# Causal masks as TensorE matmuls, and an instruction order read from a table

## The chip, the core and the metric

The kernel runs on one core of a Trainium2 chip. Its engines are TensorE (PE: matmuls; its weight loads are listed apart as PEld), VectorE (DVE), ScalarE (ACT), GpSimd (POOL) and SyncE (SP, which issues the DMAs). Each works through its own queue strictly in order. The metric is the device time of one execution in microseconds; a time for a kernel is the median of several executions.

## The reference

```python
scores = scale * q @ k.T                          # 4 batches, 8 heads, 576 positions, 64 wide
mask = pos[:, None] // 64 >= pos[None, :] // 64   # causal by blocks of 64
attn = softmax(where(mask, scores, -1e9)); a = attn @ v
x = a.transpose(0, 2, 1, 3).reshape(2304, 512)
h = x @ w_in;  g = h * tanh(softplus(h));  x = g @ w_out    # Mish; 512 -> 2048 -> 512
h = maximum(x @ w_in2, 0);  out = (h * h) @ w_out2          # 512 -> 2048 -> 512
```

## The kernel before

**Work and passes.** Attention feeds a first two-matrix layer (Mish) and that feeds a second (squared ReLU). The 2304 tokens are cut into six chunks of 384, and the two layers run as twelve passes of one chunk each, in the order of `PASSES`: (layer 0, chunk 0), (0,1), (0,2), (1,0), (0,3), (1,1), (0,4), (0,5), (1,2), (1,3), (1,4), (1,5). A pass has 16 steps `f`. In each, `first_half` (L1156) makes one 128x384 tile `hp` of the hidden layer with 12 matmuls, ScalarE turns it into `h` (L1162), `g_parts` splits `h` into an f16 high and a low part (the high one on ScalarE, L981, or GpSimd, L982; the low one on VectorE, L692), and `second_half` (L1222) adds 12 matmuls into four accumulators. All operands but those of pass (0,0) are such pairs of f16, so that a product takes three matmuls. Pass (0,0) is computed in fp32 (`first_full`, L1176, Mish at L1181; `second_full`, L1191).

**Weights.** They come from DRAM in an 8-byte format. `decode` (L1000 to L1013) fetches a block `raw` and makes f32 `wf` of it, `weigh` (L1025, L1028) finds column norms with a square on ScalarE and a small matmul, `split` makes an f16 pair `wn` (L981 and L692) and writes it to DRAM (L1056). `weights` (L1073) fetches the pairs back into a ring of three buffers `ws` when a pass needs them.

**Attention.** For each pair of heads and each tile of 128 queries, `scores` (matmul at L780) issues six f16 matmuls into a PSUM tile `spare`: two heads, each with a sum of three products. A tile of queries spans two blocks, so its first 64 rows must not see the last 64 keys: VectorE overwrites these with a memset (L832; for the tile `i == 2`, that of the last queries' tail too, L835). Then `peak` (L788) takes the maximum, `expo` (L796) the exponentials, `finish` the f16 pair `pb` of the probabilities (L815 and, through `stt`, L692), which L819 transposes by DMA. `attention_lo` does the first queries of each head in fp32 and has its own memset (L918). `settle` (L891) puts the result into `xs`, `chunk_scale` (L1098 to L1122) makes the pair `x` of it (L1105 and L692) and the norms `nsq` (L1118 and L1119 on VectorE, then a matmul at L1120) that a pass needs before its first `h`.

**What sets the order.** The program records tasks (`sch.add`), each with an engine, a list of engines to choose from (`choose`), an estimated duration and the buffers it touches. `Sched.run` then runs a list scheduler (`forward`, `backward`) with estimated times; the 140 numbers of `SHIFT` pull single groups of tasks ahead or push them back. What comes out is the order of the instructions on every engine and the engine of each task with a choice. Mish and the exponential use different tables on ScalarE, so that a change from one to the other puts an `ACT_TABLE_LOAD` ahead of it. The rings (`Ring`) give a tile one of a fixed number of buffers in the order of recording; ring `us` (the weights' scales) has eight.

Of the kernel before, what the change touches and what calls it, by code (L numbers as in the profile page):

```python
# [85 lines left out]
SHIFT = {  # L86
    ('att', 0, 0): -9100, ('att', 0, 1): 69600, ('att', 0, 2): -8000, ('att', 0, 3): -7800,
    ('att', 0, 4): 2800, ('att', 0, 5): -3000, ('att', 0, 6): 43100, ('att', 0, 7): -16100,
    ('att', 1, 0): -20200, ('att', 1, 1): 38800, ('att', 1, 2): 23300, ('att', 1, 3): -42600,
    ('att', 1, 4): 51000, ('att', 1, 5): 600, ('att', 1, 6): 98300, ('att', 1, 7): 101100,  # L90
    ('att', 2, 0): 600, ('att', 2, 1): -300, ('att', 2, 3): 600, ('att', 3, 0): 7000,
    ('att', 3, 1): 500, ('att', 3, 2): 11400, ('att', 3, 3): 19000, ('att', 4, 0): -8500,
    ('att', 4, 1): 42600, ('att', 4, 2): 90600, ('att', 4, 3): 37600, ('att', 5, 0): -45800,
    ('att', 5, 1): 36700, ('att', 5, 2): -13200, ('att', 5, 3): 27200, ('av', 0, 0): -27300,
# [8 lines left out]
    ('decode', 0, 0, 1): -17200, ('decode', 0, 0, 2): 36800, ('decode', 0, 0, 3): 40300, ('decode', 0, 0, 4): -28500,  # L103
    ('decode', 0, 0, 5): 1400, ('decode', 0, 0, 6): -1100, ('decode', 0, 0, 7): -1300, ('decode', 0, 1, 0): 29500,
    ('decode', 0, 1, 1): 84600, ('decode', 0, 1, 2): 118100, ('decode', 0, 1, 3): -29600, ('decode', 0, 1, 4): -33900,
    ('decode', 0, 1, 5): -500, ('decode', 0, 1, 6): 2200, ('decode', 0, 1, 7): 400, ('decode', 1, 0, 0): 87300,
    ('decode', 1, 0, 1): -45900, ('decode', 1, 0, 2): 29600, ('decode', 1, 0, 3): 49200, ('decode', 1, 0, 4): 8500,
    ('decode', 1, 0, 5): -12600, ('decode', 1, 0, 6): -13400, ('decode', 1, 0, 7): 6700, ('decode', 1, 1, 0): -48800,
    ('decode', 1, 1, 1): -13400, ('decode', 1, 1, 2): -11700, ('decode', 1, 1, 3): -22400, ('decode', 1, 1, 4): -900,
    ('decode', 1, 1, 5): -8200, ('decode', 1, 1, 6): -1200, ('decode', 1, 1, 7): -2700, ('norm', 0, 1): -1300,  # L110
    ('norm', 0, 2): 18300, ('norm', 0, 3): -40400, ('norm', 0, 4): -86200, ('norm', 0, 5): -27500,
    ('norm', 1, 0): -800, ('norm', 1, 1): 43900, ('norm', 1, 2): -54900, ('norm', 1, 3): 24300,
    ('norm', 1, 4): -51600, ('norm', 1, 5): -60300, ('norms', 0, 0, 0): -400, ('norms', 0, 0, 4): -8900,
    ('norms', 0, 1, 0): -2200, ('norms', 0, 1, 4): -700, ('norms', 1, 0, 0): 1100, ('norms', 1, 0, 1): -23000,
    ('norms', 1, 0, 2): -8000, ('norms', 1, 0, 3): -300, ('norms', 1, 0, 4): 600, ('norms', 1, 0, 5): 800,
    ('norms', 1, 0, 6): -7400, ('norms', 1, 0, 7): -7300, ('norms', 1, 1, 0): 400, ('norms', 1, 1, 1): 30300,
    ('norms', 1, 1, 2): -8600, ('norms', 1, 1, 3): 2000, ('norms', 1, 1, 4): -9700, ('norms', 1, 1, 5): 14900,
    ('norms', 1, 1, 6): -12700, ('norms', 1, 1, 7): -20900, ('scale', 0, 1): -24700, ('scale', 0, 2): 400,
    ('scale', 0, 3): 31000, ('scale', 0, 4): -76700, ('scale', 0, 5): 31400, ('scale', 1, 0): -15400,
    ('scale', 1, 1): 300, ('scale', 1, 2): -30100, ('scale', 1, 3): -57800, ('scale', 1, 4): -12900,  # L120
    ('scale', 1, 5): -32100, ('split', 0, 0, 0): -26300, ('split', 0, 0, 1): -204500, ('split', 0, 0, 2): -68800,
    ('split', 0, 0, 3): -45600, ('split', 0, 0, 4): 27600, ('split', 0, 0, 5): 10500, ('split', 0, 0, 6): -1900,
    ('split', 0, 0, 7): 71500, ('split', 0, 1, 0): -47000, ('split', 0, 1, 1): -87900, ('split', 0, 1, 2): -5100,
    ('split', 0, 1, 3): 3700, ('split', 0, 1, 4): 79200, ('split', 0, 1, 5): 19000, ('split', 0, 1, 6): -2100,
    ('split', 0, 1, 7): 37100, ('split', 1, 0, 0): 58400, ('split', 1, 0, 1): 28400, ('split', 1, 0, 2): -7900,
    ('split', 1, 0, 3): 79300, ('split', 1, 0, 4): 11600, ('split', 1, 0, 5): -19400, ('split', 1, 0, 6): 3300,
    ('split', 1, 0, 7): -95400, ('split', 1, 1, 0): 24600, ('split', 1, 1, 1): -14200, ('split', 1, 1, 2): 24000,
    ('split', 1, 1, 3): -22100, ('split', 1, 1, 4): 22200, ('split', 1, 1, 5): 34400, ('split', 1, 1, 6): -86300,
    ('split', 1, 1, 7): -31800, ('weigh', 0, 0, 0): -50200, ('weigh', 0, 0, 1): -89800, ('weigh', 0, 0, 2): -39300,
    ('weigh', 0, 0, 3): -15300, ('weigh', 0, 0, 4): -13700, ('weigh', 0, 0, 5): 7900, ('weigh', 0, 0, 6): 9100,  # L130
    ('weigh', 0, 0, 7): 41100, ('weigh', 0, 1, 0): -56500, ('weigh', 0, 1, 1): -52200, ('weigh', 0, 1, 2): -10400,
    ('weigh', 0, 1, 3): 9300, ('weigh', 0, 1, 4): -29400, ('weigh', 0, 1, 5): -144800, ('weigh', 0, 1, 6): -24400,
    ('weigh', 0, 1, 7): -118800, ('weigh', 1, 0, 0): -27700, ('weigh', 1, 0, 1): 62600, ('weigh', 1, 0, 2): 25700,
    ('weigh', 1, 0, 3): -48500, ('weigh', 1, 0, 4): -1000, ('weigh', 1, 0, 5): 4000, ('weigh', 1, 0, 6): 77300,
    ('weigh', 1, 0, 7): 13100, ('weigh', 1, 1, 0): -100, ('weigh', 1, 1, 1): -2000, ('weigh', 1, 1, 2): 13300,
    ('weigh', 1, 1, 3): -26100, ('weigh', 1, 1, 4): -53300, ('weigh', 1, 1, 5): -33400, ('weigh', 1, 1, 6): 4800,
    ('weigh', 1, 1, 7): 142400,
# [1408 lines left out]
```

## Time and profile before

| | us |
| --- | --- |
| three executions | 954.25, 955.18, 955.38 |
| median | 955.18 |
| the profiled execution | 952.69 |
| its span in the trace | 950.9 |
| TensorE busy in it | 903.7 |
| VectorE busy | 593.8 |
| ScalarE busy | 623.3 |

The profiled execution's own time is 1.8 us more than the span of its trace, and 2.5 us less than the median. The rows below are of that one execution. In rows in order of time the columns are start, duration, engine, line, operation, out<-in; a bracket at the end is the idle time before it and what ended it.

### The profile page before, as it was taken

Reading aid. Unit: us, or ns where it says so; the run is one execution under the profiler, and the core shown is the slowest. Engines: PE = TensorE matmul, PEld = TensorE weight load, DVE = VectorE, ACT = ScalarE, POOL = GpSimd, SP = SyncE. Lnnn points to the kernel's source line nnn. Section 1 sums busy time; section 2 is a strip of 40 time slices with the busy share of each in tenths; the row PEclk is TensorE's granted clock in tenths of the full one; section 3 lists DMA queues with packets and bytes.
Section 4 is the critical chain, followed back from the end, with each engine's and each line's share of the span. In section 5 each row is a group of like instructions: output and inputs, shape, how many; then the busy total and the mean of one; then the engine's idle time right before and its main releaser. Section 6 shows DMA issues by size and latency. Waiting matters only on the chain. (4 is left out here: it accounts for less than half of the span.)

```text
span 950.9 us, 15602 instructions
## 1 busy us (share of the span) xinstructions
PE 903.7 (95%) x5674; PEld 530.6 (56%) x5674; DVE 593.8 (62%) x1449; ACT 623.3 (66%) x1166; POOL 103.0 (11%) x133
## 2 busy tenths in 40 slices
PE   7799997897989899999999999999999999999997
PEld 6455553454555555556556555555566666666664
DVE  6789999998999996453863387677751251331211
ACT  6789799999789876554894477577752242444442
POOL 0000101211223130000210021111200000000000
PEclk9899999799999999999999999999999999999999
DMA  9657586788768798493664268597642222333430
GB/s 344 242 183 291 200 205 165 175 258 241 287 206 250 257 251 248 135 245 115 179 158 124 101 145 236 167 251 173 178 123 74 69 70 68 109 135 133 166 112 33
DMA packets 141773, 168.79 MB, mean 178 GB/s; under 512 B 105856, under 2 KB 110976, under 8 KB 137600
## 3 DMA queue, kind: packets, MB, share of 16 engines
q1 hardware_dynamic: 141696, 167.80, 60.2%
q8 instruction: 44, 0.72, 0.3%
q14 instruction: 33, 0.27, 0.1%
HBM read 125.30 MB, written 17.30 MB: 150 GB/s over the span
## 5 line engine op out<-in xcount | busy, mean ns | idle before, releaser
L692 DVE SCALAR_TENSOR_TENSOR g<-h,cst,g 128x384 f16<-128x384 f32 x176 | 110.9, 632 | 250.1 <-ACT g L981 231.9
L1162 ACT ACTIVATE h<-hp,cst 128x384 f32<-128x384 f32 x176 | 101.4, 578 | 221.2 <-PE hp L1156 219.9
L1222 PE MATMUL acc<-g,ws 128*128 128x384 f16 x1128 | 231.3, 327 | 0.7 <-DVE g L692 0.7
L1222 PE MATMUL acc<-g,raw 128*128 128x384 f16 x984 | 206.9, 327 | 0.1
L1156 PE MATMUL hp<-x,first 128*128 128x384 f16 x768 | 162.9, 335 | 6.9 <-ACT h L1162 5.5
L1222 PEld LDWEIGHTS <-ws 128*128 128x128 f16 x1128 | 109.2, 98 | 75.6 <-issue 4.1
L1156 PEld LDWEIGHTS <-first 128*128 128x128 f16 x960 | 93.6, 99 | 82.6 <-issue 25.6
L1222 PEld LDWEIGHTS <-raw 128*128 128x128 f16 x984 | 95.6, 98 | 64.5 <-issue 1.6
L1156 PE MATMUL hp<-x,raw 128*128 128x384 f16 x552 | 118.7, 327 | 0.0
L982 POOL TENSOR_SCALAR g<-h,cst 128x384 f16<-128x384 f32 x66 | 54.8, 831 | 333.0 <-ACT h L1162 106.2
L1156 PE MATMUL hp<-x,ws 128*128 128x384 f16 x408 | 86.9, 331 | 0.8 <-DMA ws<-wspill 0.8
L1156 PEld LDWEIGHTS <-raw 128*128 128x128 f16 x648 | 60.9, 98 | 45.2 <-issue 6.3
L692 DVE SCALAR_TENSOR_TENSOR pb<-pad,st,pb 128x384 f16<-128x384 f32 (+2 forms) x96 | 70.9, 754 | 11.5 <-ACT pb L815 11.3
L815 ACT ACTIVATE pb<-pad,st 128x384 f16<-128x384 f32 (+2 forms) x96 | 64.9, 712 | 18.1 <-DVE st L808 4.9
L981 ACT ACTIVATE g<-h,cst 128x384 f16<-128x384 f32 x110 | 67.4, 613 | 10.9 <-PE acc L1222 8.6
L796 ACT ACTIVATE pad<-spare,st,sq 128x448 f32<-128x448 f32 (+1 forms) x96 | 65.3, 681 | 11.8 <-DVE st L791 6.1
L1156 PEld LDWEIGHTS <-ws 128*128 128x128 f16 x504 | 48.4, 99 | 35.1 <-issue 2.9
L1176 PE MATMUL hp<-xs,first 128*128 128x384 f32 x128 | 54.8, 523 | 4.0 <-ACT h L1181 4.0
L788 DVE TENSOR_REDUCE st<-spare 128x2 f32<-128x896 f32 (+1 forms) x48 | 47.6, 992 | 0.9 <-PE spare L780 0.8
L1167 ACT ACTIVATE h<-h 128x384 f32<-128x384 f32 x85 | 43.7, 515 | 1.1
L780 PE MATMUL spare<-q 64*128 64x448 f16 (+2 forms) x384 | 39.1, 310 | 3.3 <-ACT xs L891 1.7
L1156 PE MATMUL hp<-late,first 128*128 128x384 f16 x192 | 41.6, 327 | 0.0
(225 smaller groups left out, 1158.4 us busy)
## 6 DMA issues: line engine op xcount, KB each, us to landing
ws<-wspill SPq DMA_DIRECT2D x68, 512.0 KB, 4.1
raw<-wspill SPq DMA_DIRECT2D x68, 512.0 KB, 4.0
raw<-in_w_dram SPq DMA_DIRECT2D x27, 1024.0 KB, 5.4
wspill<-wn SPq DMA_DIRECT2D x24, 512.0 KB, 4.3
qk<-in_qp_dram SPq DMA_DIRECT2D x16, 480.0 KB, 4.5
pad<-in_w_dram SPq DMA_DIRECT2D x5, 1024.0 KB, 7.3
vs<-in_va_dram SPq DMA_DIRECT2D x16, 320.0 KB, 3.8
out_dram<-ev SPq DMA_DIRECT2D x24, 192.0 KB, 2.7
```

The costliest lines, as they stand in the source:

```text
L692: return sch.add("DVE", c_dve(n) + 62 * ap, lambda: nc.vector.scalar_tensor_tensor(dst(), a(), s() if ap else s, c(), op0, op1), r=r, w=w, ...
L780: nc.tensor.matmul(out=pp.t[:, hd, o:o + k1 - k0], lhsT=qh.t[rows, u, a:a + 128], rhs=qh.t[rows, w, nq + k0:nq + k1], start=p == 0, stop=p ...
L788: sch.add("DVE", c_dve(2 * (o1 - o0)), lambda: nc.vector.reduce_max(both(st, j, r0), pp.t[r0:, :, o0:o1], axis=AX.X), w=[(pp, 0), (st, j)])
L796: t = sch.add("ACT", c_act(o1 - o0, True, 3), lambda hd=hd: nc.scalar.activation(pf[hd].t[r0:, k0:k0 + o1 - o0], pp.t[r0:, hd, o0:o1], AF. ...
L815: sch.add("ACT", c_act(n, False, 1), lambda pb=pb, pv=pv, s=s: nc.scalar.activation(pb.t[:, 0:i + 1, 0, :], pv(), AF.Copy, scale=s()), r=[ ...
L981: "ACT": ("ACT", c_act(n, False, 1), lambda: nc.scalar.activation(dst(0), src(), AF.Copy, scale=s()), False),
L982: "POOL": ("POOL", c_pool(n, False), lambda: nc.gpsimd.tensor_scalar(dst(0), src(), s(), 1.0, ALU.mult, ALU.mult), False),
L1156: nc.tensor.matmul(out=hp.t[:, 0:n], lhsT=w.t[:, f % 2, a, 128 * k:128 * k + 128], rhs=x.t[:, c, k, 0:n], start=k == 0 and i == 0, stop=k ...
L1162: sch.add("ACT", c_act(n, True, 1), lambda: nc.scalar.activation(h.t[:, 0:n], hp.t[:, 0:n], (AF.Mish, AF.Relu)[l], scale=hs()), r=[(cst, ( ...
L1167: "ACT": ("ACT", c_act(n), lambda: nc.scalar.activation(hv(), hv(), AF.Square), False),
L1176: nc.tensor.matmul(out=hp.t[:, 0:n], lhsT=wf.t[:, 512 * (f % 2) + 128 * k:512 * (f % 2) + 128 * k + 128], rhs=xs.t[:, k, 0:n], start=k == ...
L1222: nc.tensor.matmul(out=acc.t[:, 0:n], lhsT=wo.t[:, f % 2, a, 128 * m:128 * m + 128], rhs=g.t[:, c, 0:n], start=f == 0 and i == 0, stop=f = ...
```

## The change

First, the masks. The 64 memsets on VectorE are gone. Instead each score group that holds masked columns ends with one matmul per head: weights `above` (128x128 bf16, ones in the columns of the first 64 rows and zeros else) times one column of -1e24, broadcast over the 64 masked columns. It adds a large negative number to the first 64 rows and nothing to the others. The hi heads get 96 such matmuls of 64 columns, in 48 groups, `attention_lo` gets 16 of 128 columns.

Second, the order. `SHIFT` is empty, and `run` returns the order that a table `PLAN` holds: for each place the task that stands there and its engine. The list scheduler isn't run. The table changes the order on every engine and the choice of engines. Third, ring `us` has six buffers for eight.

```diff
-SHIFT = {
-    ('att', 0, 0): -9100, ('att', 0, 1): 69600, ('att', 0, 2): -8000, ('att', 0, 3): -7800,
...
-}
+SHIFT = {}
+
+PLAN = (
+    "c-p<13B1kay2qb)tz{l#i%q7=nDLlpR^&)U#xkXZGA5-==_t)nk{nVrA*ri_>f{iTkeSGAV{i7(W@Bggzt8>t|L=coyYBtmQ}>>8?bh1=^$ySbywC7^e$QS-"
...
+    def planned(self):
+
+        raw = zlib.decompress(base64.b85decode(PLAN))
+        n = len(self.tasks)
+        assert len(raw) == 3 * n
+        seq = [self.tasks[i + int.from_bytes(raw[2 * i:2 * i + 2], "little", signed=True)] for i in range(n)]
+        for i, t in enumerate(seq):
+            name = ("PE", "ACT", "DVE", "POOL", "SP")[raw[2 * n + i]]
+            t.start, t.fillers = float(i), None
+            t.eng, t.dur, t.fn, t.lock = [o for o in t.opts if o[0] == name][0] if t.opts else t.first
+            assert t.eng == name and all(d.start is not None and d.start < i for d in t.deps | t.after)
+        return seq
+
     def run(self, order):
         self.build(order)
+        if PLAN:
+            return self.planned()
...
-    R["us"] = sb("us", [128, 2 * NGRP], F32, 8)
+    R["us"] = sb("us", [128, 2 * NGRP], F32, 6)
...
+    above = cp.tile([128, 128], BF16, name="above")
+    nc.vector.memset(above[:, 0:64], 1.0)
+    nc.vector.memset(above[:, 64:128], 0.0)
+    never = cp.tile([128, 2], BF16, name="never")
+    nc.vector.memset(never, -1e24)
...
-        def scores(i, pp, o, k0, k1):
+        def scores(i, pp, o, k0, k1, mask=True):
...
-                                         start=p == 0, stop=p == 2)
-
-            steps.append(sch.add("PE", 3 * (c_mm16(k1 - k0) + 16), mm, r=[(qh, (p, j)) for p in range(2) for j in range(2)], w=[(pp, 0)]))
+                                         start=p == 0, stop=p == 2 and not mask)
+                for hd in range(2 if mask else 0):
+                    nc.tensor.matmul(out=pp.t[:, hd, o + k1 - k0 - 64:o + k1 - k0], lhsT=above, rhs=never[:, 0:1].to_broadcast([128, 64]), start=False, stop=True)
+
+            steps.append(sch.add("PE", 3 * (c_mm16(k1 - k0) + 16) + (110.0 if mask else 0.0), mm, r=[(qh, (p, j)) for p in range(2) for j in range(2)], w=[(pp, 0)]))
...
-            sch.add("DVE", 110.0, lambda pp=pp, n=n: nc.vector.memset(pp.t[0:64, :, n - 64:n], -1e25), w=[(pp, 0)])
             peak(st, 0, pp, 0, 0, n)
             if i == 2:
-                sch.add("DVE", 110.0, lambda pp=pp, n=n: nc.vector.memset(pp.t[0:64, :, n + 64:n + 128], -1e25), w=[(pp, 0)])
...
-        scores(4, pp, 0, 0, 448)
+        scores(4, pp, 0, 0, 448, False)
...
-                nc.tensor.matmul(out=pp.t[:, o:o + m], lhsT=qs.t[:, q:q + 128], rhs=qs.t[:, k:k + m], start=True, stop=True)
...
+                nc.tensor.matmul(out=pp.t[:, o:o + m], lhsT=qs.t[:, q:q + 128], rhs=qs.t[:, k:k + m], start=o == 0, stop=False)
+            nc.tensor.matmul(out=pp.t[:, 128:256], lhsT=above, rhs=never[:, 0:1].to_broadcast([128, 128]), start=False, stop=True)
...
-        sch.add("DVE", 135.0, lambda: nc.vector.memset(pp.t[0:64, 128:256], -1e9 / scale), w=[pp])
```

The lines of the changed kernel are other ones: L1215 there is L1162 here, L851 is L796, L870 is L815, L1034 is L981, L1078 is L1025, L944 is L891, L1171 and L1172 are L1118 and L1119, L843 is L788, L745 is L692, L874 is L819, L1126 is L1073, L1109 is L1056, L1053 is L1000. The numbers in names count a tile's buffer and its uses.

What the table moves is shown at three places. The first is ScalarE at the Mish of steps 11 and 12 of pass (0,1), `h_27` and `h_28`, which stand among the attention of a later chunk. Before:

```order
L1162 ACT_TABLE_LOAD
L1162 ACTIVATE h_27_1900<-hp1_132,cst_0_912 128x384
L796 ACT_TABLE_LOAD
L796 ACTIVATE pad_130,st_26_1670<-spare_133,st_26_1670,sq_3_1290 128x448
L796 ACTIVATE pad_130,st_26_1670<-tl_3_1660,st_26_1670,sq_3_1290 128x128
L796 ACTIVATE pad_130,st_26_1670<-spare_133,st_26_1670,sq_3_1290 128x448
L796 ACTIVATE pad_130,st_26_1670<-tl_3_1660,st_26_1670,sq_3_1290 128x128
L1025 ACTIVATE wsq_23_1972,us_9_1973<-wf_69 128x1024
L981 ACTIVATE wn0_66<-wf_69,us_7_1737 128x1024
L815 ACTIVATE pb_127<-pad_130,st_26_1670 128x5x128 x2
L1162 ACT_TABLE_LOAD
L1162 ACTIVATE h_28_2002<-hp0_131,cst_0_912 128x384
```

After:

```order
L851 ACTIVATE pad_130,st_26_1673<-spare_133,st_26_1673,sq_3_1274 128x448
L851 ACTIVATE pad_130,st_26_1673<-tl_3_1651,st_26_1673,sq_3_1274 128x128
L851 ACTIVATE pad_130,st_26_1673<-spare_133,st_26_1673,sq_3_1274 128x448
L870 ACTIVATE pb_127<-pad_130,st_27_1753 128x4x128 x2
L1034 ACTIVATE wn0_66<-wf_69,us_7_1759 128x1024
L1215 ACT_TABLE_LOAD
L1215 ACTIVATE h_27_1924<-hp1_132,cst_0_893 128x384
L870 ACTIVATE pb_127<-pad_130,st_26_1673 128x5x128
L1078 ACTIVATE wsq_23_1969,us_9_1970<-wf_69 128x1024
L944 ACTIVATE xs_3_1279<-spare_133,sv_2_937 128x384
L1215 ACTIVATE h_28_1985<-hp0_131,cst_0_893 128x384
```

The four exponentials and two of the steps behind them have moved ahead of `h_27`, and one table load serves `h_27` and `h_28`, where each had its own. Over the stretch from the first to the 38th Mish of L1162 the table loads go from 27 to 19, the high parts of `g` on ScalarE from 5 to 14 and those of `x` (L1105) from 7 to 9.

The second place is VectorE at the norms `nsq_1`, those of chunk 0 for pass (1,0), early in pass (0,1). Before, up to L1119, on which the norm's matmul L1120 waits:

```order
L760 TENSOR_SCALAR sq_3_1290<-sq_3_1290 128x2
L836 COPY tl_2_1338<-spare_133 128x256
L692 SCALAR_TENSOR_TENSOR pb_127<-pad_130,st_21_1152,pb_127 128x4x128
L788 TENSOR_REDUCE st_23_1342<-tl_2_1338 128x2
L761 SCALAR_TENSOR_TENSOR sq_3_1290<-sq_3_1290 128x1
L1118 TENSOR_TENSOR nsq_1_1308<-nsq_1_1308,wsq_18_1321 128x768
L762 TENSOR_SCALAR sq_3_1290<-sq_3_1290 128x1
L1145 TENSOR_SCALAR cst_0_912<-wst_0_662,cst_0_912 128x16
L1119 TENSOR_TENSOR nsq_1_1308<-nsq_1_1308 128x384
```

After, from the first addition of the norms on:

```order
L1171 TENSOR_TENSOR nsq_1_1294<-nsq_1_1294,wsq_18_1307 128x768
L846 TENSOR_SCALAR st_22_1312<-st_22_1312,sq_2_1085 128x2
L745 SCALAR_TENSOR_TENSOR x1_73<-xs_2_1149,cst_1_1215,x1_73 128x384
L889 COPY tl_2_1327<-spare_133 128x256
L1195 TENSOR_TENSOR cst_0_893<-cst_0_893,wst_0_638 128x1
L811 TENSOR_SCALAR sq_3_1274<-spare_133 128x2
L745 SCALAR_TENSOR_TENSOR wn0_66<-late_70,us_3_838,wn0_66 128x1024
L745 SCALAR_TENSOR_TENSOR x1_73<-xs_2_1149,cst_1_1215,x1_73 128x384
L812 TENSOR_SCALAR sq_3_1274<-sq_3_1274 128x2
L1196 TENSOR_SCALAR cst_0_893<-cst_0_893 128x1
L1087 TENSOR_SCALAR wst_1_1071<-spare_133 128x2
L1172 TENSOR_TENSOR nsq_1_1294<-nsq_1_1294 128x384
```

L1118 (now L1171) stood three rows ahead of L1119 (now L1172); it has moved ahead, and ten rows stand between the two, among them two low parts of `x1`, a low part of `wn` and a step (L1087) that reads the small matmul L1028. On TensorE the norm's matmul stood right behind a score group; now the twelve matmuls of pass (0,1)'s next step and that small matmul stand in between.

The third place is SyncE's queue, also in pass (0,1), around two fetches of `ws` for its last steps. Before:

```order
L819 DMA_TRANSPOSE late_70<-pb_127 128x6x128 x2
L1073 DMA ws_65<-wspill0_63 128x2048
L1000 DMA raw0_67<-in_w2_dram 128x1024
L1073 DMA ws_65<-wspill0_63 128x2048
L1056 DMA wspill1_64<-wn0_66 128x2048
L819 DMA_TRANSPOSE late_70<-pb_127 128x8x128 x2
L1000 DMA raw1_68<-in_w2_dram 128x1024
L742 DMA qk_111<-in_qp_dram 128x960
L1056 DMA wspill1_64<-wn0_66 128x2048
L819 DMA_TRANSPOSE late_70<-pb_127 128x10x128 x2
L1073 DMA ws_65<-wspill0_63 128x2048
```

After:

```order
L874 DMA_TRANSPOSE late_70<-pb_127 128x6x128
L1053 DMA raw1_68<-in_w2_dram 128x1024
L874 DMA_TRANSPOSE late_70<-pb_127 128x8x128
L1109 DMA wspill1_64<-wn0_66 128x2048
L874 DMA_TRANSPOSE late_70<-pb_127 128x8x128
L874 DMA_TRANSPOSE late_70<-pb_127 128x10x128 x2
L1126 DMA ws_65<-wspill0_63 128x2048
L1109 DMA wspill1_64<-wn0_66 128x2048
L1053 DMA raw0_67<-in_w2_dram 128x1024
L1126 DMA ws_65<-wspill0_63 128x2048
```

Two fetches of weights (L1073) stood among the transposes of `pb` (L819), ahead of those of 8 and 10 blocks; now both stand behind all of these. Each fetch is issued about 3 us of matmul work ahead of the step that reads it, where it was about 14.

## Rows read from the trace of the kernel before

**Rows 1.** The page: TensorE busy us, share of the span, instructions.
```profile
PE 903.7 (95%) x5674; PEld 530.6 (56%) x5674; DVE 593.8 (62%) x1449; ACT 623.3 (66%) x1166; POOL 103.0 (11%) x133
```

**Rows 2.** Busy by stretch: length; PE, PEld, DVE, ACT, POOL; clock; DMA share; GB/s.
```profile
0.00:150.00 150.00, 135.37 (x576) 82.62 (x577) 125.91 (x331) 122.20 (x262) 6.36 (x17) 0.97 0.73 246
150.00:350.00 200.00, 176.11 (x1171) 99.79 (x1169) 187.48 (x442) 179.66 (x284) 46.17 (x50) 0.95 0.79 231
350.00:700.00 350.00, 346.45 (x2417) 200.42 (x2415) 213.95 (x538) 224.77 (x447) 45.44 (x58) 1.00 0.68 175
```

**Rows 3.** Whom TensorE waited for, whole run: us in total, times, longest us.
```profile
PE hp L1120 <- DVE nsq L1119: 6.5, 1, 6.5
PE hp L1156 <- ACT h L1162: 5.5, 6, 2.5
PE hp L1176 <- ACT h L1181: 4.0, 2, 3.6
```

**Rows 4.** TensorE in order of time, 212 to 270 us: two stalls behind h.
```profile
224.04 2.11 PE L1156 MATMUL hp<-x,first 128*128 128x384 f16 x12 [1.89 <-ACT h L1162]
...
233.62 0.65 PE L1156 MATMUL hp<-x,first 128*128 128x384 f16 x3 [2.52 <-ACT h L1162]
```

**Rows 5.** ScalarE in order of time, around the same two stalls.
```profile
222.11 1.28 ACT L1162 ACT_TABLE_LOAD   x1
...
231.69 1.28 ACT L1162 ACT_TABLE_LOAD   x1
```

**Rows 6.** ScalarE groups, 150 to 350 us: busy, mean ns.
```profile
L1162 ACT ACT_TABLE_LOAD x14 | 18.0, 1283 | 0.3
```

**Rows 7.** VectorE memsets of line 832 in two stretches: length, busy (count), clock.
```profile
150.00:350.00 200.00, 1.49 (x9) 0.95 0.79 231
350.00:700.00 350.00, 3.13 (x19) 1.00 0.68 175
```

**Rows 8.** The same for line 835.
```profile
150.00:350.00 200.00, 0.82 (x5) 0.95 0.79 231
350.00:700.00 350.00, 1.49 (x9) 1.00 0.68 175
```

**Rows 9.** VectorE in order of time, last steps before the longest stall.
```profile
165.70 0.82 DVE L788 TENSOR_REDUCE st<-spare 128x2 f32<-128x640 f32 x1
...
170.06 0.35 DVE L1119 TENSOR_TENSOR nsq<-nsq 128x384 bf16<-128x384 bf16 x1
```

**Rows 10.** TensorE in order of time, that stall.
```profile
170.46 0.48 PE L1120 MATMUL hp<-nsq,ones 128*128 128x384 bf16 x1 [6.45 <-DVE nsq L1119]
```

**Rows 11.** TensorE in order of time, the stall at 46 us.
```profile
46.40 1.55 PE L1176 MATMUL hp<-xs,first 128*128 128x384 f32 x2 [3.59 <-ACT h L1181]
```

**Rows 12.** ScalarE in order of time, ahead of it.
```profile
43.42 1.13 ACT L1007 ACTIVATE first<-raw 128x1024 f32<-128x1024 f32 x1
```

**Rows 13.** Busy by stretch, columns as in Rows 2.
```profile
25.00:50.00 25.00, 18.77 (x73) 11.44 (x74) 19.72 (x44) 18.20 (x46) 0.00 (x0) 0.80 0.64 241
```

**Rows 14.** TensorE in order of time: two 1-column matmuls ahead of large ones.
```profile
214.09 0.19 PE L1028 MATMUL spare<-us,onesq 128*128 128x1 bf16 x2
214.14 0.65 PE L1156 MATMUL hp<-x,first 128*128 128x384 f16 x3
214.63 0.65 PE L1222 MATMUL acc<-g,ws 128*128 128x384 f16 x3
```

**Rows 15.** TensorE in order of time: a score group, then the next matmul.
```profile
675.66 0.74 PE L780 MATMUL spare<-q 64*128 64x448 f16 x6
676.34 0.66 PE L1156 MATMUL hp<-x,raw 128*128 128x384 f16 x3
```

**Rows 16.** The page: parts of g on ScalarE; weight loads beside matmuls of line 1222.
```profile
L1222 PEld LDWEIGHTS <-ws 128*128 128x128 f16 x1128 | 109.2, 98 | 75.6 <-issue 4.1
...
L981 ACT ACTIVATE g<-h,cst 128x384 f16<-128x384 f32 x110 | 67.4, 613 | 10.9 <-PE acc L1222 8.6
```

**Rows 17.** Weight fetches of line 1073: issue to landing.
```profile
DMA to landing us min/median/max: 3.1/4.1/9.7
```

More of the change, by code (lines that the diff above doesn't have):

```diff
@@ L1 @@
+import base64
 import heapq
+import zlib
 from contextlib import ExitStack
@@ L83 @@
 C0_AT, C1_AT, A_AT = 40000.0, 85000.0, [[0.0, 20000.0], [70000.0, 90000.0], [95000.0, 150000.0]]
-SHIFT = {
-    ('att', 0, 0): -9100, ('att', 0, 1): 69600, ('att', 0, 2): -8000, ('att', 0, 3): -7800,
[L88 to L94, printed above, removed]
[8 rows of a table removed]
[L103 to L137, printed above, removed]
-}
@@ L208, in add @@
         t.deps, t.succ, t.pos, t.idx = set(deps), [], pos, len(self.tasks)
-        t.after, t.before, t.rows, t.final, t.fillers, t.banks = set(), [], 1.0, None, None, None
+        t.start, t.after, t.before, t.rows, t.final, t.fillers, t.banks = None, set(), [], 1.0, None, None, None
         for acc, write in ((r, False), (w, True)):
@@ L913, in mm_s @@
             for q, o, k, m in ((0, 0, 448, n), (256, n, 448, n), (128, 2 * n, 384, 64)):
-                nc.tensor.matmul(out=pp.t[:, o:o + m], lhsT=qs.t[:, q:q + 128], rhs=qs.t[:, k:k + m], start=True, stop=True)
-        steps = [sch.add("PE", 2 * c_f32(192) + c_f32(64), mm_s, r=[qs], w=[pp])]
+                nc.tensor.matmul(out=pp.t[:, o:o + m], lhsT=qs.t[:, q:q + 128], rhs=qs.t[:, k:k + m], start=o == 0, stop=False)
+            nc.tensor.matmul(out=pp.t[:, 128:256], lhsT=above, rhs=never[:, 0:1].to_broadcast([128, 128]), start=False, stop=True)
+        steps = [sch.add("PE", 2 * c_f32(192) + c_f32(64) + 80.0, mm_s, r=[qs], w=[pp])]
         t1 = lambda: pp.t[:, 0:384].rearrange("p (h s) -> p h s", h=2)
-        sch.add("DVE", 135.0, lambda: nc.vector.memset(pp.t[0:64, 128:256], -1e9 / scale), w=[pp])
         sch.add("DVE", c_dve(384), lambda: nc.vector.reduce_max(st.t[:, 0:2], t1(), axis=AX.X), w=[pp, (st, 0)])
```

80 lines of the change are left out of this document (added), and 8 rows, old and new, of the table SHIFT.

## Prediction

> **What bounds the kernel now.** Read the busy times first. TensorE is busy 95% of the span [rows 1], so over most of it the kernel is bound by matmuls, and time can be won only where TensorE idles. The table by stretch shows where that is [rows 2]: in the first 150 us it is busy 135.37, idle 14.6; from 150 to 350 us it is busy 176.11, idle 23.9; from 350 to 700 us busy 346.45, idle 3.6. So the place is the stretch from 150 to 350 us. There VectorE is busy 187.48 of 200 us and ScalarE 179.66, while both fall to 214 and 225 of 350 us behind it. Three engines are nearly full at once, and what decides is how well their orders fit. The list of waits names whom TensorE waited for [rows 3]: once 6.5 us for VectorE's norms, six times for a Mish `h` (5.5 us), twice for a Mish of the fp32 pass (4.0 us).
>
> Then go to these waits in time. At 224.04 and 233.62 us TensorE stood 1.89 and 2.52 us for an `h` [rows 4]; on ScalarE a table load of 1.28 us begins at 222.11 and at 231.69, right ahead of these two Mish [rows 5]. At 170.46 us the norm's matmul had waited 6.45 us [rows 10]: VectorE began to reduce a score tile at 165.70 and reached the second addition of the norms only at 170.06, 4.4 us later, a full queue and not a missing operand [rows 9]. At 46.40 us the fp32 pass had waited 3.59 us for its Mish [rows 11], ahead of which ScalarE had put a decode step of 1.13 us [rows 12].
>
> **The change part by part.** All sums are against the profiled execution's own 952.69 us, which is 2.5 us below the median of 955.18.
>
> *The memsets.* In the stretch that counts they are 1.49 us in 9 of line 832 [rows 7] and 0.82 us in 5 of line 835 [rows 8], 2.31 us of VectorE's 187.48; it would go to 185.2. Behind 350 us 19 and 9 memsets go, on an engine that is busy 214 of 350 us: nothing, the cover being its idle time there.
>
> *The order in the stretch from 150 to 350 us.* ScalarE gives up 8 table loads between the first and the 38th Mish. By the loads' mean of 1283 ns [rows 6] that is 10.3 us. Against it stand 9 high parts of `g` and 2 of `x` that come to ScalarE; by 613 ns for a part of `g` [rows 16] they cost 6.7 us. Net it loses 3.6 us of 179.66. One of the loads that goes is the one ahead of `h_28`, thus the one at 231.69 in front of the 2.52 us stall. The stall at 170.46 is cut in another way: VectorE does not do the second addition sooner (ten rows now stand between the two additions, and I put them at about the same 4.4 us), but TensorE has twelve more matmuls, some 2 us, to do ahead of the norm's matmul. So part of that wait goes and part of it stays. How much the stretch gains is bounded from both sides. If only the memsets count, it gains 2.3 us. If the new order closes every gap of VectorE, the stretch shortens to VectorE's 185.2 us, a gain of 14.8. TensorE's 176.1 us lie below that, so VectorE would be the bound. No row is near to either end: 6.5 and 5.5 us of the idle time are named stalls of which the order touches the larger part, the rest is small waits. I take the middle, **-8.5**.
>
> The Trainium skill, ScalarE: Activation LUTs, section "Table sets: the hidden batching unit", puts a change of table at about 2.7 us with a drain in it, and advises to put functions of one set together. The trace shows less: the load from 222.11 takes 1.28 us and the stall behind it is 1.89 us. By that page the eight loads would be an estimated 21.6 us and not 10.3; the stretch would still end with VectorE's 185.2, so it moves the sum towards its far end and not past it.
>
> *The stall at 46.40 us.* The decode step no longer stands ahead of the first Mish. At least its 1.13 us go. At most the whole 3.59 us go, and some of the slow clock: over 25 to 50 us the granted clock was 0.80 [rows 13], 0.20 x 25 = 5.0 us of lost clock, of which I give a third, 1.7, to the time behind this stall. The ends are -1.1 and -5.3; I take the middle, **-3.2**, no row being nearer to one.
>
> *The masks on TensorE.* Where TensorE idles, before 350 us, 20 score groups and the 16 units of the low heads get their masks under 23.9 and 14.6 us of idle time; I count nothing, and about 3 us if that cover were gone. Behind 350 us TensorE has none: 28 groups with two masks each (19 and 9 memsets there [rows 7, 8]) lie on the path. Low end: three 384-column matmuls start 0.49 us apart from the next three [rows 14], 0.163 each, so 64 columns are 27 ns; and two 1-column matmuls cost 0.05 us together there, so a small matmul is no dearer. Two masks are 0.054 us, 28 pairs 1.5 us. High end: each mask brings a weight load of 98 ns [rows 16]; if it isn't hidden, a pair costs 2 x (98 + 27) = 0.25 us, 28 pairs 7.0. Between them: a score group took 0.68 us to the next matmul [rows 15], where its three pairs of 448 columns (0.19 each) make 0.57. So 0.11 us goes with entering and leaving a group, and it is paid already; the masks add a second change of weights' shape within it. I take 0.1 us a pair, nearer to the low end because a load beside a stream of matmuls is seen hidden (98 ns under every 163): **+2.8**.
>
> *The rest.* From 350 to 700 us 3.6 us of idle time is all that an order could win there: **-1.0**, between 0 and -3.6. Behind 700 us the order is the same. Ring `us` with six buffers frees space and can only add a wait; scales are small and written long before the last reader, so nothing, its cover being the order that already knows of the six. The table itself costs no time on the chip.
>
> The sum: -8.5 - 3.2 + 2.8 - 1.0 = -9.9; 952.69 - 9.9 = 942.8 for an execution like the profiled one, and with the 2.5 us by which the median lies above it, **945.3**.
>
> **The rivals.**
>
> *The masks' weight loads are exposed.* Then 28 pairs cost 0.15 more than I took, +4.2, and before 350 us 20 pairs at 0.25 and 16 single ones at 0.15 are 7.4 us, of which half would find no idle time, +3.7: 953.2, at the edge of no change. For it speaks that a mask's 64 columns are shorter than its load; against it the spacing of the 1-column matmuls [rows 14], whose weights also changed. The Trainium skill, TensorE: Matmul & The Clock Gate, Part 3, "The mechanism", says a weight load overlaps matmuls in flight only when the row groups differ, which speaks for this rival. The trace disagrees for full-height weights: 98 ns loads lie beside 128-row matmuls that follow each other by 163 ns.
>
> *The stalls move but stay.* VectorE stays full, other gaps open, and only the certain parts count: -2.3 - 1.1 + 2.8 = -0.6, so 954.6. For it speaks that VectorE had 94% in the stretch and loses only 1% of its work.
>
> *The other side: weights come late.* On SyncE two fetches now stand behind four transposes, and are issued about 3 us of matmul work ahead of their reader. A fetch takes 3.1 us at best, 4.1 in the median and 9.7 at worst [rows 17]. At the median it costs 1.1 us each, which the range of the stretch holds. At the worst it would be 5.6 us more; three of them make 16.8 and 962.1. It decides from 9.9 us of lateness in all, where the gain is gone. Against it: TensorE waited for a fetch hardly at all before, and SyncE may run ahead of TensorE.
>
> *Everything fits.* The stretch at its end of -14.8, the early stall at -5.3, the waits behind 350 at -3.6: 934.1.
>
> **How the numbers follow.** My forecast, faster by about 1%, 0.60, with a range of its own of 938 to 952.5: the half-widths 6.3 for the stretch, 2.1 for the early stall, about 2 for the masks and 1.5 for the waits make 7.1 when added as independent. Exposed loads 0.10, stalls stay 0.09, late weights 0.12, everything fits 0.09. From 934 to 955 leaves out the late weights and about half of the last case, under 2 in 10. A measurement of this kernel tells about 0.2% from no change, so faster means below 953.3 and slower above 957.1. Faster: the forecast, half of the exposed loads and everything fits, 0.74. Within: the other half and the stalls that stay, 0.14. Slower: 0.12.
>
> **What the profile after would show.** Right: TensorE's idle time from 150 to 350 us falls from 23.9 to about 15 with VectorE still the fullest beside it; the waits for `h` lose most of 5.5 us; the norm's wait falls to about 4; the stall at 46 us shrinks below 2. ScalarE's table loads fall by about 8 in the stretch. A masked score group behind 350 us lasts about 0.1 us longer to the next matmul. Wrong: groups longer by 0.25 mean exposed loads; waits of matmuls for `ws` of several us mean late weights; VectorE at 185 busy in a stretch as long as before means that the stalls only moved. Most of all the forecast falls if the gain of the stretch lies outside 2.3 to 14.8, or if the order changes something in the first 150 us, where 14.6 us of idle time stand and I priced only one stall.

## The result and the profile after

The changed kernel takes 941.05 us (median of four executions, 938.26 to 942.76), the kernel before 954.71 in its four: ratio 0.9854, 95% interval 0.9828 to 0.988. That is 13.7 us less, where 9.9 was forecast, and 941.05 lies within the range of 934 to 955 and within the narrower one of 938 to 952.5. The profiled execution took 941.45, with a span of 939.4 us, 11.5 less than before.

The page's row of busy times, to be held against [rows 1]:

```profile
PE 901.2 (96%) x5786; PEld 532.3 (57%) x5786; DVE 574.7 (61%) x1386; ACT 618.9 (66%) x1177; POOL 82.5 (9%) x114
```

The table by stretch, columns as in [rows 2]:

```profile
0.00:150.00 150.00, 137.72 (x657) 84.50 (x658) 132.26 (x336) 132.63 (x285) 8.38 (x20) 1.00 0.71 247
150.00:350.00 200.00, 183.62 (x1240) 104.99 (x1241) 174.07 (x406) 171.25 (x280) 28.15 (x34) 0.97 0.77 231
350.00:700.00 350.00, 345.47 (x2448) 201.85 (x2447) 208.81 (x523) 224.86 (x451) 41.99 (x54) 1.00 0.69 178
```

TensorE's idle time is 12.3, 16.4 and 4.5 us, where it was 14.6, 23.9 and 3.6. That is 9.0 us less over the span. Its busy time falls by 2.5 us although it has 112 matmuls more, and the column of the clock says why: 1.00 and 0.97 for 0.97 and 0.95. Over the span the mean granted clock went from 0.984 to 0.994; (1 - 0.984) x 950.9 = 15.2 us of lost clock have become (1 - 0.994) x 939.4 = 5.6. Idle time and lost clock can't be added up, since TensorE also idles in some of the slow stretches.

The stretch of [rows 13], 25 to 50 us, after the change:

```profile
25.00:50.00 25.00, 24.29 (x123) 14.98 (x124) 23.44 (x49) 22.13 (x49) 0.00 (x0) 1.00 0.81 295
```

TensorE was busy 18.77 of these 25 us at a clock of 0.80, and is busy 24.29 at 1.00. The first Mish of the fp32 pass ends at 38.6 us, before at 46.4.

Two later points compare the same work: the first and the 41st `h` of L1162 (L1215 after the change), the first `h` of pass (0,1) and the ninth of pass (1,0). ScalarE, two rows before the change and two after:

```profile
154.13 0.58 ACT L1162 ACTIVATE h<-hp,cst 128x384 f32<-128x384 f32 x1
...
360.37 0.56 ACT L1162 ACTIVATE h<-hp,cst 128x384 f32<-128x384 f32 x1
```

```profile
145.74 0.58 ACT L1215 ACTIVATE h<-hp,cst 128x384 f32<-128x384 f32 x1
...
346.38 0.56 ACT L1215 ACTIVATE h<-hp,cst 128x384 f32<-128x384 f32 x1
```

The changed kernel is 8.4 us ahead at the first of them and 14.0 at the second. At the last of the 176, which end at 938.2 and 926.8 us, it is 11.4 ahead. So it wins 8.4 us early and 5.6 in the middle stretch, and gives 2.6 back behind it.

The list of waits, to be held against [rows 3] (only the rows that answer to it, and the new one):

```profile
PE hp L1209 <- ACT h L1215: 3.8, 4, 1.4
PE hp L1173 <- DVE cst L1029: 3.1, 1, 3.1
...
PE acc L1275 <- DMA ws<-wspill: 1.6, 1, 1.6
```

The wait for the fp32 pass's Mish is gone from the list (4.0 us in all before). That for `h` fell from 5.5 to 3.8, that for the norm from 6.5 to 3.1, and a fetch of weights costs 1.6 us.

### The profile page after: what moved, and what is told of

It is laid out like the page before. It is cut to its first block, busy times and chain, and to the rows that moved or that the text cites. A ratio compares the mean times of both kernels' runs of the same rounds, so it can differ in the third digit from the quotient of the medians.

```text
span 939.4 us, 15711 instructions
## 1 busy us (share of the span) xinstructions
PE 901.2 (96%) x5786; PEld 532.3 (57%) x5786; DVE 574.7 (61%) x1386; ACT 618.9 (66%) x1177; POOL 82.5 (9%) x114
## 5 line engine op out<-in xcount | busy, mean ns | idle before, releaser
L745 DVE SCALAR_TENSOR_TENSOR g<-h,cst,g 128x384 f16<-128x384 f32 x176 | 108.0, 617 | 233.5 <-ACT g L1034 222.7
L1215 ACT ACTIVATE h<-hp,cst 128x384 f32<-128x384 f32 x176 | 101.1, 577 | 216.4 <-PE hp L1209 211.1
L1275 PE MATMUL acc<-g,raw 128*128 128x384 f16 x984 | 204.6, 326 | 0.0
L1209 PE MATMUL hp<-x,first 128*128 128x384 f16 x768 | 157.8, 330 | 3.8 <-ACT h L1215 3.8
L1209 PE MATMUL hp<-x,ws 128*128 128x384 f16 x408 | 85.0, 328 | 0.0
L745 DVE SCALAR_TENSOR_TENSOR pb<-pad,st,pb 128x384 f16<-128x384 f32 (+2 forms) x96 | 72.0, 756 | 20.2 <-ACT pb L870 20.1
L1034 ACT ACTIVATE g<-h,cst 128x384 f16<-128x384 f32 x123 | 75.1, 612 | 13.3 <-PE acc L1275 12.5
L870 ACT ACTIVATE pb<-pad,st 128x384 f16<-128x384 f32 (+2 forms) x96 | 66.7, 711 | 15.0 <-DVE st L863 4.9
L851 ACT ACTIVATE pad<-spare,st,sq 128x448 f32<-128x448 f32 (+1 forms) x96 | 65.2, 680 | 15.8 <-DVE st L846 9.2
L1035 POOL TENSOR_SCALAR g<-h,cst 128x384 f16<-128x384 f32 x53 | 43.1, 815 | 342.5 <-PE acc L1275 129.7
L843 DVE TENSOR_REDUCE st<-spare 128x2 f32<-128x896 f32 (+1 forms) x48 | 47.8, 996 | 11.4 <-PE spare L836 9.5
L1229 PE MATMUL hp<-xs,first 128*128 128x384 f32 x128 | 49.5, 495 | 0.1
```

The lines of the kernel that those rows point to most:

```text
L745: return sch.add("DVE", c_dve(n) + 62 * ap, lambda: nc.vector.scalar_tensor_tensor(dst(), a(), s() if ap else s, c(), op0, op1), r=r, w=w, ...
L843: sch.add("DVE", c_dve(2 * (o1 - o0)), lambda: nc.vector.reduce_max(both(st, j, r0), pp.t[r0:, :, o0:o1], axis=AX.X), w=[(pp, 0), (st, j)])
L851: t = sch.add("ACT", c_act(o1 - o0, True, 3), lambda hd=hd: nc.scalar.activation(pf[hd].t[r0:, k0:k0 + o1 - o0], pp.t[r0:, hd, o0:o1], AF. ...
L870: sch.add("ACT", c_act(n, False, 1), lambda pb=pb, pv=pv, s=s: nc.scalar.activation(pb.t[:, 0:i + 1, 0, :], pv(), AF.Copy, scale=s()), r=[ ...
L1034: "ACT": ("ACT", c_act(n, False, 1), lambda: nc.scalar.activation(dst(0), src(), AF.Copy, scale=s()), False),
L1035: "POOL": ("POOL", c_pool(n, False), lambda: nc.gpsimd.tensor_scalar(dst(0), src(), s(), 1.0, ALU.mult, ALU.mult), False),
```

## The experiments

Each kernel reads its order from a table like that of the change, so that single parts of order and masks could be set apart. Of such a table the diffs show nothing but its place. Times are medians, each with its ratio to the kernel before in the same session (954.83, 954.27 and 955.32 us in the three sessions). Ring `us` has eight buffers in the five kernels with the old order or a part of it and in the order alone, six in the others; no run changes only that, so its share isn't shown.

**Masks alone: the old order with TensorE masks.**

```diff
 SHIFT = {}
 PLAN = (
...
-    R["us"] = sb("us", [128, 2 * NGRP], F32, 6)
+    R["us"] = sb("us", [128, 2 * NGRP], F32, 8)
```

> The instructions stand as in the kernel before, on the same engines, from a table made of its own order; only the masks are the new matmuls (ring us has eight buffers). Theory (the order makes the time, the masks cost some 0.1 us a group behind 350 us and free 2.3 us of VectorE): 952.4 to 957.5, about +0.5 against before. Rival, the masks' weight loads are exposed: +4 to +8, 959 to 963. Rival, the freed VectorE is what gained: 941 to 946.

Measured: 950.25 us, ratio 0.9954 (0.9934 to 0.9974). All three were missed: the masks alone are worth about 4.4 us, neither nothing nor the whole gain. The one profiled execution was the slowest of the nine (953.13) and does not show where they come from.

**Order alone: the new order with memsets.**

```diff
             scores(i, pp, 0, 0, n)
...
+            sch.add("DVE", 110.0, lambda pp=pp, n=n: nc.vector.memset(pp.t[0:64, :, n - 64:n], -1e25), w=[(pp, 0)])
             peak(st, 0, pp, 0, 0, n)
```

The other memsets are back as well, and no mask is left on TensorE.

> The new order with the masks as memsets on VectorE, each right ahead of the instruction that reads the masked tile; TensorE has no masks. Theory: the order alone carries the gain, VectorE loses 2.3 us of it in the stretch from 150 to 350 us and TensorE wins back 2.8 us behind it: 938 to 943. Rival, the order needs the VectorE time that the memsets took: 946 to 952.

Measured: 954.43 us, ratio 0.9992 (0.9971 to 1.0014), no change from before. The theory fell, and further than the rival went: the order alone carries no gain. With the TensorE masks the same order gains 13.7 us. So the two parts do not add: alone they are worth 4.4 us and 0.8, the latter within its interval of nothing, together 13.7. The order was made without memsets, and other places for them in it were not tried.

**Halves of the order.**

```diff
 PLAN = (
...
-    R["us"] = sb("us", [128, 2 * NGRP], F32, 6)
+    R["us"] = sb("us", [128, 2 * NGRP], F32, 8)
```

> TensorE masks; the new order up to the first matmul of pass (0,1), about 146 us, the old order for all the rest. Theory, from the profile after (the first Mish of pass (0,1) ends 8.4 us earlier): 945 to 950. Rival, the early part is worth the 3.2 us of the prediction: 950 to 955. Rival, the early gain is lost again because the later order waits for something else: 954 or more.

> The reverse: TensorE masks, the old order up to the first matmul of pass (0,1), the new one from there. Theory, from the profile after (some 7 us won between that point and 350 us, some 4 us given back behind it): 949 to 954. Rival, by the prediction's -8.5 and +1.8: 946 to 949. Both halves together should give the gain of the whole change, 13.7 us, counted against the first experiment.

Measured: 947.57 us (0.9911 to 0.9944) for the new order first, 951.25 (0.9949 to 0.9975) for the old one first. Both are within what the theory gave, but against the masks alone (950.25) they gain 2.7 and lose 1.0, the latter within the intervals, and together not the 9 that separate masks alone from the whole change. A third cut shows what cuts do.

> TensorE masks; new order up to the fourth pass after the fp32 one begins to lose its lead (Mish 56, about 350 us), then the old order. Theory: what the changed kernel gives back behind 350 us (14.0 us ahead there, 11.4 at the end, by the profiles) is the new order's waits and not the masks, since masks in the old order cost 0.3 us there: 937 to 940. Rival, it is the masks: 941. Rival, the old order waits at the seam: 944 or more.

Measured: 949.84 us (0.9924 to 0.9966), 9 us slower than the changed kernel. Its list of waits from 330 to 380 us:

```profile
PE spare L832 <- ACT pad L850: 11.2, 1, 11.2
```

One wait of 11.2 us stands at the seam: a score group of the old order comes before ScalarE, which is elsewhere in the new one, has emptied the PSUM tile. So the cuts measure their seams too, and no share of the gain follows from these three kernels.

**Which memsets.**

```diff
-                nc.tensor.matmul(out=pp.t[:, o:o + m], lhsT=qs.t[:, q:q + 128], rhs=qs.t[:, k:k + m], start=o == 0, stop=False)
-            nc.tensor.matmul(out=pp.t[:, 128:256], lhsT=above, rhs=never[:, 0:1].to_broadcast([128, 128]), start=False, stop=True)
+                nc.tensor.matmul(out=pp.t[:, o:o + m], lhsT=qs.t[:, q:q + 128], rhs=qs.t[:, k:k + m], start=True, stop=True)
...
+        sch.add("DVE", 135.0, lambda: nc.vector.memset(pp.t[0:64, 128:256], -1e9 / scale), w=[pp])
```

> The new order with the 16 masks of the low heads as memsets on VectorE again; the high heads keep their TensorE masks. Theory, from the new order with all memsets, whose first Mish came 6 us later than in the changed kernel at a granted clock of 0.86 in 25 to 50 us: these 16 memsets make TensorE idle early and the clock falls, 946 to 950. Rival, the high heads' memsets in the stretch from 150 to 350 us carry the whole loss: 940 to 943.

> The reverse: low heads masked on TensorE, the 48 masks of the high heads as memsets on VectorE, new order. Theory: the early gain stays, the stretch from 150 to 350 us loses 4 to 7 us, the masks behind 350 us are no gain on TensorE: 945 to 949. Rival, the memsets are worth only their own 2.3 us and TensorE wins 2.8 us behind 350 us: 939 to 942.

Measured: 944.13 us (0.9861 to 0.9905) with the low heads' memsets, 949.73 (0.992 to 0.9964) with the high heads'; against the changed kernel's ratio that is 2.8 and 8.4 us. The first lies just below what the theory gave, the second just above. The first kernel shows the clock. Rows of TensorE by 2 us (stretch, length, busy, clock, DMA share, GB/s), first of the kernel before, ahead of its slow clock and in it:

```profile
26.00:28.00 2.00, 0.63 (x4) 1.00 0.97 374
28.00:30.00 2.00, 0.98 (x7) 0.87 0.59 193
32.00:34.00 2.00, 2.00 (x6) 0.50 0.59 193
```

The new order with the low heads' memsets:

```profile
20.00:22.00 2.00, 0.73 (x7) 1.00 1.04 361
22.00:24.00 2.00, 1.15 (x7) 1.00 1.04 421
26.00:28.00 2.00, 2.00 (x11) 0.50 0.40 87
```

The changed kernel, at the same places:

```profile
20.00:22.00 2.00, 1.33 (x9) 1.00 1.05 374
22.00:24.00 2.00, 1.78 (x14) 1.00 1.05 412
26.00:28.00 2.00, 2.00 (x18) 1.00 0.53 169
28.00:30.00 2.00, 2.00 (x18) 1.00 0.99 283
```

In the kernel before TensorE idles 2.4 us between 26 and 30 us, with the low heads' memsets 2.1 us between 20 and 24; both then work at half the clock, 1.2 for 2.4 GHz, for some 7 us. In the changed kernel it idles 0.9 us from 20 to 24 us, and the clock stays. An idle piece of this size alone doesn't settle it, as a later row of the changed kernel shows, with 1.7 us idle and the clock at 1.00:

```profile
54.00:56.00 2.00, 0.29 (x2) 1.00 0.93 299
```

The first Mish ends at 43.6 us with the low heads' memsets. In the old order with TensorE masks it ends at 45.0, in the new order with all memsets at 44.7. It takes both parts to come to 38.6.

The profiles of all fourteen kernels, one each, say the same of two stretches. Early: in the eight that start in the new order and have no memset in the low heads the first Mish ends between 38.0 and 39.0 us, at a clock of 1.00 from 25 to 50 us; one of the eight is the kernel below that has no masks at all, so what counts is that VectorE has no memset there, and not the new matmuls. In the other six it ends between 43.6 and 46.4, at a clock of 0.80 to 0.93. From the first to the 41st `h`: in the six kernels that are in the new order there, with the high heads masked on TensorE, it takes 197.8 to 200.6 us. In the old order it takes 204.5 to 206.3 (four kernels), in the new order with the high heads' memsets 205.4 and 202.5, and without any masks 204.0, which stays unexplained (the kernel cut at 350 us is left out, its seam lies there). So in these profiles the middle gain, too, comes only with order and masks together.

The second kernel keeps the early part up to the first Mish (38.8 us, clock 1.00) and loses elsewhere. Its row from 350 to 700 us, in a profiled execution that was the slowest of its eleven:

```profile
350.00:700.00 350.00, 338.27 (x2344) 196.05 (x2343) 215.25 (x549) 222.42 (x447) 41.79 (x54) 1.00 0.70 176
```

TensorE idles 11.7 us there, and the largest entry of its waits in that stretch is the transposes of `pb`:

```profile
PE spare L932 <- DMA late<-pb: 5.3, 4, 2.3
```

In the changed kernel these are 2.4 us there. How much of this is that execution's own bad luck, one profile doesn't tell.

**The decode step ahead of the first Mish**, moved away in the old order with TensorE masks, and put back in the new one:

```diff
 PLAN = (
...
```

> The old order with TensorE masks as in the first experiment, but the decode step of 1.13 us that stood ahead of the first Mish stands behind the second. Theory (the stall at 46 us had this step ahead of it): the stall shrinks by some 1.1 us, against the first experiment 1 to 2 us less, 948 to 949.5. Rival, the stall is no matter of this step: 950 or more. Rival, the clock recovers with it: 944 to 946.

> The changed kernel, but one decode step (1.13 us on ScalarE, with the VectorE step behind it) stands directly ahead of the first Mish again, as it did before. Theory (the step is worth its own 1.1 us and not the clock): the first Mish ends about 1 us later, granted clock stays 1.00 from 25 to 50 us, time 941 to 943. Rival, the step brings back the stall of 3 us and the slow clock: 946 to 950.

Measured: 949.74 us (0.9931 to 0.9968), within noise of the 950.25 of masks alone, and 942.04 (0.9836 to 0.9879), within noise of the changed kernel's 941.05. The waits for the fp32 pass's Mish, first masks alone, then with the step moved away:

```profile
PE hp L1228 <- ACT h L1233: 3.7, 2, 3.3
```

```profile
PE hp L1228 <- ACT h L1233: 2.6, 2, 2.3
```

In the old order the step is worth 1.0 us, about its length of 1.13; put back in the new one it delays the end of the first Mish by 0.4 us, from 38.6 to 39.0, less than expected. It makes neither the rest of that stall nor the clock: from 25 to 50 us the clock was 0.80 with the step moved away in the old order, and 1.00 with it put back in the new one.

**The price of a mask.**

```diff
-                for hd in range(2 if mask else 0):
+                for hd, r in ((0, 0), (1, 0), (0, 1), (1, 1), (0, 2), (1, 2), (0, 3), (1, 3)) if mask else ():
-                    nc.tensor.matmul(out=pp.t[:, hd, o + k1 - k0 - 64:o + k1 - k0], lhsT=above, rhs=never[:, 0:1].to_broadcast([128, 64]), start=False, stop=True)
+                    nc.tensor.matmul(out=pp.t[:, hd, o + k1 - k0 - 64:o + k1 - k0], lhsT=above, rhs=never[:, 0:1].to_broadcast([128, 64]), start=False, stop=r == 3)
```

> The changed kernel with every mask matmul of the high heads issued four times (eight small matmuls a group). Theory, a small matmul costs its 27 ns of columns where TensorE is full: six more in 28 groups, 4.5 us, and little of the 20 groups ahead, 944 to 947. Rival, 0.05 us each as predicted: 8.4 us, 949 to 951. Rival, exposed loads at 0.125 us each: 21 us or more, 960 and up.

Measured: 946.81 us (0.9891 to 0.9929), 5.4 us above the changed kernel by the ratios, as the first theory had it. The other kernel leaves the masks out:

```diff
-                for hd in range(2 if mask else 0):
+                for hd in range(0):
...
-            nc.tensor.matmul(out=pp.t[:, 128:256], lhsT=above, rhs=never[:, 0:1].to_broadcast([128, 128]), start=False, stop=True)
```

> The changed kernel without any masking: no mask matmuls, no memsets (the masked keys are not left out of the softmax). Theory (from the old order, where the masks cost 0.3 us from 350 us on): the masks are nearly free, 939.5 to 941.5. Rival, the prediction's 0.1 us a pair: 938 to 938.5, 2.8 less behind 350 us. Rival, exposed weight loads: 930 to 934.

Measured: 944.25 us (0.9856 to 0.9916), not faster than with the masks; all three guesses missed it on the low side. TensorE in order of time, the changed kernel, a masked group and an unmasked one:

```profile
659.71 0.74 PE L833 MATMUL spare<-q 64*128 64x448 f16 x6
660.38 0.23 PE L836 MATMUL spare<-never,above 128*128 128x64 bf16 x2
660.46 0.65 PE L1209 MATMUL hp<-x,raw 128*128 128x384 f16 x3
...
664.94 0.74 PE L833 MATMUL spare<-q 64*128 64x448 f16 x6
665.61 0.66 PE L1209 MATMUL hp<-x,raw 128*128 128x384 f16 x3
```

Six score matmuls take 0.67 us to the next start in both; the two masks add 0.08 us. With eight masks:

```profile
664.50 0.74 PE L833 MATMUL spare<-q 64*128 64x448 f16 x6
665.17 0.42 PE L836 MATMUL spare<-never,above 128*128 128x64 bf16 x8
665.43 0.65 PE L1209 MATMUL hp<-x,raw 128*128 128x384 f16 x3
```

Eight take 0.26 us, so six more cost 0.18, 0.03 each: the columns, and no weight load. The loads themselves, all 384 of this kernel's high heads:

```profile
L836 PEld LDWEIGHTS <-above 128*128 128x128 bf16 x384 | 14.4, 98 | 11.8 <-issue 10.2
```

Each is listed at 98 ns, but together they fill 14.4 us, 0.04 each: they overlap one another. Without masks TensorE is busy 343.17 us from 350 to 700 us, 2.3 less than with them, which is 28 pairs at 0.08:

```profile
350.00:700.00 350.00, 343.17 (x2393) 199.31 (x2391) 211.93 (x529) 225.90 (x453) 42.28 (x54) 1.00 0.71 179
```

It did no other work in that time: 2393 matmuls stand against 2448, about the 56 masks less. From the 41st `h` to the last the kernel takes 580.3 us without masks and 579.8 with them. In this profile TensorE's 2.3 us went into waits, then.

**The fetches of weights.**

```diff
 PLAN = (
...
```

> The changed kernel, but the two fetches of weights that stand behind four transposes on SyncE stand ahead of the last three of them. Theory (the profile after shows one wait of 1.6 us for such a fetch at 232 us, issued 8.6 us earlier): the wait goes, time the same or up to 2 us less, 938.5 to 941. Rival, the transposes that come later cost as much: 941 to 943.

Measured: 941.67 us (0.9832 to 0.9875), the same as the changed kernel. The late fetch is there, SyncE and TensorE of the changed kernel:

```profile
223.66 0.41 SPq L1126 DMA_DIRECT2D ws<-wspill  x1
```

```profile
232.33 1.96 PE L1275 MATMUL acc<-g,ws 128*128 128x384 f16 x11 [1.61 <-DMA ws<-wspill]
```

Issued at 223.66, it is waited for until 232.33. With the fetches ahead that wait is gone from the list, but the transposes come later. TensorE of that kernel:

```profile
223.11 0.45 PE L931 MATMUL spare<-late,vs 128*64 128x384 f16 x1 [2.83 <-DMA late<-pb]
224.18 3.08 PE L931 MATMUL spare<-late,vs 128*64 128x384 f16 x29 [0.62 <-DMA late<-pb]
```

The changed kernel waited 0.2 us for them here. So the time lies where the rival put it, 941 to 943, and the wait has moved from the weights to the transposes.

## Why the prediction was right

**The stretch from 150 to 350 us, -8.5.** Between the same two `h` the stretch became 5.6 us shorter (206.2 to 200.6), inside the bounds of 2.3 and 14.8, but two thirds of the middle that I took. The table by stretch looks better than that: idle time fell by 7.5 us, and the lost clock from (1 - 0.95) x 200 = 10 to (1 - 0.97) x 200 = 6 us. But 150 to 350 us doesn't hold the same work in both, and before the change some of the slow clock fell on the long stall, where TensorE had nothing to do:

```profile
166.00:168.00 2.00, 0.00 (x0) 0.50 1.01 294
```

The term didn't price the clock at all. The fewer table loads are as forecast:

```profile
L851 ACT ACT_TABLE_LOAD x10 | 12.8, 1283 | 0.5 <-DVE cst L1183 0.3
L1215 ACT ACT_TABLE_LOAD x9 | 11.5, 1283 | 0.2
```

19 loads stand where 28 did. What bounds the stretch was not as I had it. VectorE was to stay the fullest at 185 us; it is busy 174.07 and ScalarE 171.25, while both do more in the first 150 us (132 each, before 126 and 122). The work had started earlier. The norm's wait came to 3.1 us, where I had written about 4, but for another reason than a full queue:

```profile
152.29 0.55 DVE L1171 TENSOR_TENSOR nsq<-nsq,wsq 128x768 bf16<-128x768 bf16 x1
...
159.01 0.16 DVE L1087 TENSOR_SCALAR wst<-spare 128x2 uint32<-128x2 uint32 x1 [3.18 <-ACT pad L851]
159.09 0.35 DVE L1172 TENSOR_TENSOR nsq<-nsq 128x384 bf16<-128x384 bf16 x1
```

The second addition comes 6.8 us after the first, where I had put it at about 4.4 us, and VectorE itself stands 3.18 us at L1087 between them. The small matmul that L1087 reads had been done since 156.34; what ended the wait, by the row, is ScalarE's exponential, behind a table load. TensorE and ScalarE:

```profile
156.18 0.17 PE L1081 MATMUL spare<-us,onesq 128*128 128x1 bf16 x1
```

```profile
156.97 1.28 ACT L851 ACT_TABLE_LOAD   x1
158.27 0.62 ACT L851 ACTIVATE pad<-spare,st,sq 128x320 f32<-128x320 f32 x1
```

Why that step should wait for it the rows don't say. The waits for `h` lost 1.7 of 5.5 us and not most of them.

**The stall at 46.40 us, -3.2.** This term was mis-sized, 3.2 for 8.4 us. The first Mish comes 7.8 us earlier; the stall of 3.59 us is gone altogether, and with it the slow clock ahead of and behind it. I gave a third of the 5.0 us of lost clock to this place, and all 5.0 went. TensorE up to the first Mish of pass (0,1), which ends 8.4 us earlier (146.3 for 154.7 us), before and after:

```profile
0.00:154.70 154.70, 138.69 (x597) 0.97 0.71 239
```

```profile
0.00:146.30 146.30, 134.96 (x623) 1.00 0.72 250
```

Idle time went from 16.0 to 11.3 us. These 4.7 us and the 5.0 us of clock stand beside the 8.4; TensorE has also done 26 matmuls more by then. The prediction had itself named the case on which it would fall, an order that changes something in the first 150 us, where it priced one stall out of 14.6 us of idle time. The cause that I named, the decode step, is worth 1.0. What goes with the clock that stays is that TensorE idles less between 20 and 30 us, in the low heads' attention, and there masks and order work together, in eight kernels against six. The prediction looked at the stall and not at the idle time that stood ahead of the clock's fall.

**The masks, +2.8.** Right in size on TensorE: 28 pairs at 0.08 us, 2.2. The rival of the exposed weight loads falls: a pair costs 0.08, not 0.25, and a further mask 0.03. That the sum charges them in full fails: in the old order they lengthen the way from the 41st `h` to the last by 0.3 us (577.5 for 577.2), and in the new order it is no shorter without them.

**The rest, -1.0.** From 350 to 700 us idle time rose by 0.9 us, to 4.5. It went the other way, by little. Masks and rest together were +1.8 and came to +2.6; in the kernels with the decode step put back and the fetches ahead they are 1.3 and 0.5, so that one execution moves this by about as much as the term.

**The form of the sum.** It added four terms, and the runs show that masks and order are not terms: the order alone gives nothing (0.9992), the masks alone 4.4 us, both 13.7. A forecast for either half alone by the same sum would have failed. "The stalls move but stay" is what the order does with memsets. Of the rivals, the late weights came once, at 1.6 us. "Everything fits" adds up to 934.3 and not to 934.1, which changes nothing.

**The number and its luck.** By stretches the change gave -8.4, -5.6 and +2.6 us, forecast were -3.2, -8.5 and +1.8. That their sum, -11.4, stands so near to -9.9 is luck in good part, since the first two terms were off in opposite directions. What carries 8.4 us, less idle time in the low heads and a clock that stays high, was in the forecast as one stall and a third of its slow clock. Most of what the median lies below 945.3 comes from elsewhere: I added 2.5 us because the profiled execution of the kernel before lay so far below its median, and that of the changed kernel lies 0.4 above its own.

**What stays open.** Why the masks alone gain 4.4 us in the old order, and why leaving the masks out of the new order is, if anything, slower; in its one profile the loss lies between the first and the 41st `h` (204.0 for 200.6 us), at a clock of 0.96 for 0.97 from 150 to 350 us. Both kernels spread by 6 to 10 us between executions. The median of the mean granted clock goes with part of it (0.9835 for the kernel before, 0.986 for masks alone, 0.9885 for the order alone, 0.9915 without masks, 0.9945 changed), but the high heads' memsets gave 949.73 us at 0.995, so that the clock isn't all. The cuts at 146 us do not divide the gain. What ring `us` does alone, and what of the middle stretch is the table loads, the norm or the clock, no run tells.

## What to carry to other kernels

Look for what stands ahead of the clock's fall, not only for the stall: twice here, 2.4 and 2.1 us of idle time within 4 us were followed by some 7 us at half clock, some 3.4 us lost. Compare two orders at the same work and not at the same time; a window of fixed times can show gains that were made elsewhere. Where an order was fitted to a set of instructions, price the order and the instructions together: half of such a change can be worth nothing. And a small matmul inside a group that is there anyway cost its columns only, so masking on the matmul engine was cheaper here than the step and the hand-over that it took from another engine.
